# The transposed r and k of the last eight units: 32-by-32 blocks loaded by DMA and turned on VectorE in place of turns on TensorE

## The chip, the cores and the metric

The kernel runs on one core of one Trainium2 chip. Its time is the device time of one execution in microseconds (us); lower is better. Before the change the median of three runs is 600.69 us (600.6 to 601.51).

## What is computed

The reference is a recurrent attention layer, followed by a two-layer block with the activation h - tanh(h). All data is float32: 4 batches, 8 heads, 768 steps, head size 48; the model width is 8 x 48 = 384 and the hidden width 2048.

```python
for t in range(S):
    kt, vt, rt = (k[:, :, t], v[:, :, t], r[:, :, t])
    cur = np.einsum('bhd,bhe->bhde', u[None] * kt, vt)
    y[:, :, t] = np.einsum('bhd,bhde->bhe', rt, state + cur)
    state = w[None, :, :, None] * state + np.einsum('bhd,bhe->bhde', kt, vt)
x = y.transpose(0, 2, 1, 3).reshape(B * S, H * D)
h = x @ w_in
return (h - np.tanh(h)) @ w_out
```

## The kernel before

**Units.** The attention is cut into 24 units. A unit is 64 steps of two of the four batches (all heads), so its rows fill 128 partitions: two halves of 64 steps. Units alternate between the two pairs of batches. `unit(n)` describes one of them. Its steps, with lines of the profile: load r, k and v (`fetch`, L752, on SP's queue); kw = k times a table of decay (L893, VectorE); turn r and kw on TensorE into PSUM, so that features lie on partitions (`turn`, L764, four transposes of 128x128 for each, two heads at a time); take them out of PSUM as rT (times a table of decay, `scale_r`, L768, VectorE) and kT (`copy_k`, L777, ScalarE); rk = r k u and its sum over features, du (L781, L908, L785, VectorE), which ScalarE writes on the diagonal of the tile `at` (L789); rT against the state (`from_state`, L719 through `put`); rT against kT (`levels`, L719), whose part below the diagonal VectorE copies into `at` (L918); `at` against v into y and kw against v into the new state (`outputs`, L719); y out of PSUM into the tiles xt and rest (`to_xt`, `to_rest`, L855, ScalarE); the state's update and decay (`keep` L882, L927, VectorE). GpSimd moves `rest` to its rows of xt by small DMAs (`fill`, L876).

**Late units.** The last eight units, 16 to 23 (`two`, n >= L * (FIRST + 2)), have no PSUM bank of their own for the turned r and k and for the levels. There all of it shares the tile `yk_ps` with y and the new state. So the turns of a late unit come after everything that the unit before has in `yk_ps` was read (`free`: xt, rest, add, cp, diag of the unit before).

**Dense tiles.** Two units make a block j of 256 rows of the second part; there are 12 blocks, each with 8 tiles of 256 hidden columns. A tile is: h (L168, TensorE, twelve matmul records of the profile), five functions on ScalarE (L177 to L185), four steps on VectorE (`g` L192, c1 L194, c2 L196, cp L198), and the product with w_out. From the last pass of the first blocks on, that product is done with seven half-size products in place of eight: GpSimd forms sums of g (`sums_of_g`, L242 to L246), TensorE multiplies (`products`, L257), VectorE combines (`collect`, L285). The first six blocks (FIRST) go through the hidden columns in three passes; between passes their partial results wait in the twelve `part` tiles (L224), until `gather` (L289) adds them in. The other six blocks go through in one pass, among the late units.

**The order.** The program is one list per engine, in an order that a planner (`Plan`) makes when the kernel is built. Each step is a task with an engine, a cost, the tasks it comes after and a due time. `forward` plays the plan, `backward` finds the latest times, and a random search moves due times: first 2500 tries on the part up to BUSY = 240 us, then 500 tries on the whole (L470 to L486). The plan decides the order only; at run time each engine goes through its list and waits on semaphores.

Of the kernel before, what the change touches and what calls it, by code (L numbers as in the profile page):

```python
# [11 lines left out]
F32 = mybir.dt.float32  # L12
# [4 lines left out]
ALU = mybir.AluOpType  # L17
# [13 lines left out]
SHORT = 64  # L31
# [3 lines left out]
L = 2  # L35
FIRST = 6
# [19 lines left out]
class Dims:  # L56
    def __init__(self, r, moe_w_in):
        self.B, self.H, self.S, self.D = r.shape
        self.DM, self.DFF = moe_w_in.shape
        self.NP = self.H // 2  # L60
        self.NCH = self.S // C
        self.NU = self.NCH * self.B
        self.NK = self.DM // 128
        self.NX = self.D // self.NK
        self.NF = self.DFF // 128
        self.NT = L * C
        self.NB = self.NU // L

        self.HEAD = [slice(i * PAD, i * PAD + self.D) for i in range(2)]
# [76 lines left out]
class Dense:  # L146


    def __init__(self, nc, work, gpool, ps_d, shared, out, rows, outs=None, last=None, seven=None):
        self.nc, self.work, self.gpool, self.ps_d, self.new_outs, self.seven = nc, work, gpool, ps_d, outs, seven  # L150
        self.out, self.rows, self.xts, self.sums, self.last, self.negative = out, rows, {}, {}, last, set()
        self.d, self.w_in_sb, self.w_out_sb, self.m1b, self.smallb = (
            shared[x] for x in ("dims", "w_in", "w_out", "m1b", "smallb"))
# [55 lines left out]
    def empty(self, t, i):  # L209

        whole, at = t.fs[1] == self.d.NF, (t.j, i)
        if t.fs[0]:
            t.o = part = self.sums.pop(at) if whole else self.sums[at]
            if whole and t.j == self.d.NB - 1 and self.last is not None:
                t.o = self.last[:, i]
            if i and whole and t.j in self.negative:
                self.nc.vector.tensor_tensor(t.o, part, self.outs[i], ALU.subtract)
            else:
                self.nc.vector.tensor_tensor(t.o, self.outs[i], part, ALU.add)
            return  # L220
        if whole:
            t.o = self.work.tile([128, self.d.DM], F32, name="o", tag="o")
        else:
            t.o = self.sums[at] = self.work.tile([128, self.d.DM], F32, name="part", tag="part", bufs=L * FIRST)  # L224
        if t.j == self.d.NB - 1:
            if self.last is not None:
                t.o = self.last[:, i]
            self.nc.vector.tensor_copy(t.o, self.outs[i])
        else:
            self.nc.scalar.copy(t.o, self.outs[i])  # L230
# [70 lines left out]
class Plan:  # L301
# [10 lines left out]
    BEGIN = {"PE": 1.5, "DVE": 2.2, "ACT": 1.2, "POOL": 4.3, "SP": 1.2}  # L312

    def __init__(self):
        self.tasks, self.fills = [], []

    def add(self, engine, cost, run, after=(), due=1e9, data=0, gated=False, steps=0):
        t = SimpleNamespace(engine=engine, cost=cost, run=run, after=[x for x in after if x], due=due, data=data,
                            gated=gated, steps=steps, then=[], n=len(self.tasks))
        for x in t.after:  # L320
            x.then.append(t)
        self.tasks.append(t)
        return t

    def hop(self, t, x):
        return self.NEAR_HOP if x.engine == t.engine else self.HOP
# [94 lines left out]
    def backward(self, plan):  # L421
# [25 lines left out]
                    changed.add(x.engine)  # L447
        return latest

    def order(self, first=2500, tries=500):  # L450


        due = [t.due for t in self.tasks]
        for t in reversed(self.tasks):
            for x in t.then:
                due[t.n] = min(due[t.n], due[x.n] - t.cost - self.HOP - (self.LANDS if t.data else 0))
        plan = self.forward(due)
        for _ in range(4):
            due = self.backward(plan)
            plan = self.forward(due)  # L460
        chance = Random(5)

        def moved():
            by, at, wide = chance.choice((0.3, 1, 2, 5)), chance.uniform(0, until), chance.choice((15, 40, 100, 700))
            return [x + chance.gauss(0, by) * (start is not None and abs(start - at) < wide / 2) for x, start in zip(due, plan[1])]


        until = self.BUSY
        plan = self.forward(due, until)
        for _ in range(first):  # L470
            new = moved()
            other = self.forward(new, until)
            if other[0] <= plan[0]:
                plan, due = other, new
        plan = self.forward(due)
        until = plan[0]
        for _ in range(tries):
            new = moved()
            other = self.forward(new)
            if chance.random() < .5:  # L480
                latest = self.backward(other)
                again = self.forward(latest)
                if again[0] < other[0]:
                    other, new = again, latest
            if other[0] <= plan[0]:
                plan, due = other, new  # L486
        self.due = due
        _, starts, done = plan
        self.forward(due)
        fitted, order = {n: (free, runs) for free, n, runs in self.fitted}, []  # L490
        for t in done:
            t.start = starts[t.n]
            free, runs = fitted.get(t.n, (0.0, [])) if t.engine == "PE" else (0.0, [])
            order += [SimpleNamespace(engine="PE", cost=0.0, start=free, run=run) for run in runs]
            order.append(t)
        return order
# [19 lines left out]
def near(ctx, tc, r, k, v, w, u, out, shared, moe_w_in, moe_w_out):  # L516


    nc = tc.nc
    V, A, T, G, Q = nc.vector, nc.scalar, nc.tensor, nc.gpsimd, nc.sync  # L520
    d = shared["dims"]
# [12 lines left out]
    def fixed(name, shape, dt=F32):  # L534
# [2 lines left out]
    plan = Plan()  # L537
    add = plan.add
    e_of = {"SP": Q, "ACT": A, "PE": T, "DVE": V, "POOL": G}
    dense = Dense(nc, work, gpool, ps_d, shared, out,  # L540
                  lambda n: [(n % 2 * 2 + z) * d.S + n // 2 * SHORT for z in range(2)], lambda t: new_outs(t), shared["last"])
    HALF = [slice(z * SHORT, (z + 1) * SHORT) for z in range(2)]


# [178 lines left out]
    def unit(n):  # L723
# [46 lines left out]
        def scale_k():  # L770
            t.kT = work.tile([128, NP, 2, SHORT], F32, name="kT", tag="kT")
            V.tensor_tensor(t.kT, k_ps.rearrange("d (p z t) -> d p z t", p=NP, z=2),
                            inverse[:, :, None, 1:].to_broadcast([128, NP, 2, SHORT]), ALU.mult)

        def copy_k():
            t.kT = work.tile([128, NP, 2, SHORT], F32, name="kT", tag="kT")
            A.copy(flat4(t.kT), k_ps)  # L777
# [112 lines left out]
        if two:  # L890
            free = [b1.xt, b1.rest, b1.add, b1.cp, b1.diag]
        x.turn = add("PE", .46, lambda: turn(rt, r_ps), [x.r] + free, steps=8)
        x.kw = add("DVE", .47, lambda: V.tensor_tensor(kw[:, :, :D], t.kt[:, :, :D], w_down, ALU.mult), [x.k, downs, b2.out])  # L893
        x.turn_k = x.rk = add("PE", .46, lambda: turn(t.kt if direct else kw, k_ps), [x.k if direct else x.kw] + free, steps=8)
        both = [x.turn, x.turn_k]
        x.rT = add("DVE", .62, scale_r, both + [ups])
        if direct:
            x.kT = add("DVE", .62, scale_k, both + [inverted])
            x.extra = add("POOL", .5, thirds, [x.v])
        else:  # L900
            x.kT = add("ACT", .5, copy_k, both)
        if product:
            now = add("ACT", 1.05, own_k, [x.kT, w_us])
            x.own = add("PE", .7, own_levels, [now, x.rT, b2.out], steps=64)
            x.diag = add("DVE", .64, lambda: V.copy_predicated(t.at, same.bitcast(I32)[:, None, None, :].to_broadcast([128, 2, NP, SHORT]), own_lev), [x.own, b2.out])
        else:
            x.rk = add("DVE", .47, own, [x.r, x.k, b2.du, b1.rk if not b1.own else None])
            now = add("DVE", .47, lambda: V.tensor_tensor(t.rk, t.rk, ub, ALU.mult), [x.rk, bonus])  # L908
            x.du = add("DVE", .47, own_sum, [now, b2.diag])
            now = add("ACT", 1.0, lambda: diagonal(range(0, H // 2)), [x.du, b2.out])  # L910
            x.diag = add("ACT", 1.0, lambda: diagonal(range(H // 2, H)), [now])
# [20 lines left out]
                                for kk in range(NK) for i in range(2)]  # L932


    tiles, stored = [], {}
    mixed = []

    def mixing():
# [86 lines left out]
    for part in PASSES:  # L1025
        for j in range(FIRST):
            for f in range(done, done + part, 2):
                pace = 5.2 + (14.8 / part if not done and j < FIRST - 1 else 1.25)
                hidden(j, (done, done + part), f, now, pace, done >= SEVEN)
                now += pace  # L1030
        done += part
    for n in range(L * (FIRST + 2), d.NU):
# [327 lines left out]
```

## Time and profile before

| what | before |
|---|---|
| median of three runs | 600.69 us |
| the profiled execution | 599.5 us |
| its span, first to last instruction | 597.7 us |
| L764 from 354.8 us on (the late units' turns), records | 64, 0.272 us each |
| L768 from 357.6 us on (rT of late units) | 8, 0.692 us |
| L777 from 357.0 us on (kT of late units) | 8, 0.585 us |
| L671 (reciprocal of the table, once) | 1.778 us |
| loads of r, k, v on SP (L752), shortest and median issue of r | 0.595, 0.626 us |
| r, k, v loads, issue to landing, median | 2.9, 3.4, 3.5 us |
| xt fills on GpSimd's queue, issue to landing, median | 2.2 us |

An engine's busy time is the sum of its records. Matmuls overlap in the array, so a record's length is more than what one costs in a row of them. "Idle before, releaser" gives what ended an engine's wait. `PEld` is the weight load of TensorE, which shows a wait of TensorE first. The stretches used below count from the span's start.

### The profile page before, as it was taken

How to read it: one execution, taken by the hardware profiler on the slowest of the kernel's cores; microseconds unless marked ns; L12 is line 12 of the kernel's file. 1: busy time of each engine (PE TensorE's matmuls, PEld its weight loads, DVE VectorE, ACT ScalarE, POOL GpSimd, SP SyncE). 2: the span in 40 equal slices, each digit the busy share in tenths (PEclk: the TensorE clock that was granted, in tenths of full speed). 3: DMA queues.
4: the chain of work that ended last, by engine and by line, in shares of the span. 5: the costliest groups of instructions: out<-in, count | busy, mean ns of one | idle time of the engine just before them, and what ended most of it. 6: DMA issues, size and time to landing. Idle time of an engine off the chain costs nothing.

```text
span 597.7 us, 14262 instructions
## 1 busy us (share of the span) xinstructions
PE 579.0 (97%) x5589; PEld 491.5 (82%) x5589; DVE 465.6 (78%) x781; ACT 403.0 (67%) x902; POOL 203.7 (34%) x366
## 2 busy tenths in 40 slices
PE   8879999999999999999999999999999999999996
PEld 5557677777777779899999999989889888999995
DVE  5799979999999999986777775665776775555765
ACT  3798798899668867766555563765675866556552
POOL 5002212201000324454555463442435354334620
PEclk9999999999999999999999999999999999999999
DMA  6976986935211311201110011120211200100101
GB/s 127 228 132 121 168 195 110 142 94 114 60 53 27 62 29 24 50 5 24 28 26 13 16 28 34 34 47 15 55 22 27 42 1 9 27 2 7 27 3 31
DMA packets 86325, 33.77 MB, mean 56 GB/s; under 512 B 78536, under 2 KB 80680, under 8 KB 86248
## 3 DMA queue, kind: packets, MB, share of 16 engines
q1 hardware_dynamic: 81084, 25.57, 22.0%
q0 software_dynamic: 4992, 6.99, 5.5%
q8 instruction: 46, 0.75, 0.6%
q14 instruction: 31, 0.25, 0.1%
q10 hardware_dynamic: 172, 0.20, 0.1%
HBM read 26.94 MB, written 4.72 MB: 53 GB/s over the span
## 4 chain that ended last, share of the span: by engine, by line
PE 72%; DVE 14%; ACT 5%; issue 4%; DMA 3%; SPq 2%; DVEq 0%; POOL 0%; ACTq 0%; POOLq 0%
PE h L168 34%; PE p L257 25%; PE o L206 5%; PE yk_ps L719 5%; SPq L752 2%; DVE tg L196 2%; DVE tg L194 1%; DVE g L192 1%; DVE g L198 1%; DMA vt<-in_v_dram 1%; PE yk_ps L764 1%; ACT at L789 1%; DMA kt<-in_k_dram 1%; DVE rT L768 1%; DVE mixed L266 1%
## 5 line engine op out<-in xcount | busy, mean ns | idle before, releaser
L168 PE MATMUL h<-xt,w_in_sb 128*128 128x256 f32 x1152 | 281.1, 381 | 1.9 <-DVE w_in_sb L143 0.9
L168 PEld LDWEIGHTS h<-xt,w_in_sb 128*128 128x128 f32 x1152 | 212.5, 190 | 32.7 <-DVE g L192 1.4
L242 POOL TENSOR_TENSOR sg<-g 128x256 f32<-128x256 f32 x69 | 53.1, 770 | 171.4 <-DVE g L198 105.3
L194 DVE SCALAR_TENSOR_TENSOR tg<-s,tg 128x512 f32<-128x512 f32 x96 | 69.5, 723 | 53.5 <-ACT tg L181 28.6
L257 PE MATMUL p<-mixed,sg 128*128 128x192 f32 x426 | 104.0, 326 | 0.0
L181 ACT ACTIVATE tg<-h 128x512 f32<-128x512 f32 x96 | 57.2, 596 | 55.7 <-PE h L168 55.7
L192 DVE TENSOR_TENSOR g<-h,th 128x512 f32<-128x512 f32 x96 | 66.0, 688 | 26.8 <-ACT tg L181 10.6
L177 ACT ACTIVATE s<-h 128x512 f32<-128x512 f32 x96 | 57.4, 598 | 41.4 <-PE h L168 41.3
L876 POOL DMA_DIRECT2D xt<-rest x66 | 32.3, 495 | 142.7 <-ACT rest L855 142.7
L179 ACT ACTIVATE th<-h 128x512 f32<-128x512 f32 x96 | 57.4, 598 | 33.4 <-PE h L168 33.2
L198 DVE COPY_PREDICATED g<-small,tg 128x512 f32<-128x512 int32 x96 | 75.6, 787 | 4.0
L196 DVE SCALAR_TENSOR_TENSOR tg<-q,tg 128x512 f32<-128x512 f32 x96 | 68.2, 711 | 9.8 <-ACT q L183 7.4
L257 PEld LDWEIGHTS p<-mixed,sg 128*128 128x128 f32 x426 | 75.0, 190 | 0.0
L206 PE MATMUL o<-w_out_sb,g 128*128 128x384 f32 x192 | 69.8, 490 | 1.7 <-DVE g L198 1.6
L257 PE MATMUL p<-w_out_sb,g 128*128 128x192 f32 x284 | 71.2, 332 | 0.0
L183 ACT ACTIVATE q<-s,m1b 128x512 f32<-128x512 f32 x96 | 69.7, 726 | 0.7
L185 ACT ACTIVATE small<-s,smallb 128x512 f32<-128x512 f32 x96 | 69.4, 723 | 0.3
L257 PEld LDWEIGHTS p<-w_out_sb,g 128*128 128x128 f32 x284 | 51.8, 190 | 7.1 <-DVE o L285 0.2
L789 ACT ACTIVATE at<-same,du 128x64 f32<-128x64 f32 x184 | 47.7, 342 | 5.3 <-DVE du L785 5.0
L206 PEld LDWEIGHTS o<-w_out_sb,g 128*128 128x128 f32 x192 | 35.5, 190 | 18.4 <-issue 1.9
L244 POOL TENSOR_TENSOR sg<-sg,g 128x128 f32<-128x128 f32 x69 | 43.2, 626 | 5.1
L246 POOL TENSOR_TENSOR sg<-sg,g 128x128 f32<-128x128 f32 x69 | 36.9, 534 | 5.1
(132 smaller groups left out, 688.2 us busy)
## 6 DMA issues: line engine op xcount, KB each, us to landing
st<-in_moe_w_out_dram SPq DMA_DIRECT2D x8, 768.0 KB, 5.0
rt<-in_r_dram SPq DMA_DIRECT2D x48, 96.0 KB, 2.9
vt<-in_v_dram SPq DMA_DIRECT2D x48, 96.0 KB, 3.5
st<-in_moe_w_in_dram SPq DMA_DIRECT2D x16, 288.0 KB, 5.4
kt<-in_k_dram SPq DMA_DIRECT2D x44, 96.0 KB, 3.4
out_dram<-o POOLq DMA_DIRECT2D x44, 96.0 KB, 2.1
st<-in_moe_w_in_dram POOLq DMA_DIRECT2D x16, 96.0 KB, 4.8
xt<-rest POOLq DMA_DIRECT2D x66, 16.0 KB, 2.2
```

The costliest lines, as they stand in the source:

```text
L168: self.nc.tensor.matmul(t.h2[:, z], self.w_in_sb[:, t.f // 2, kk, z * 128 : (z + 1) * 128], self.xts[t.j][:, kk].rearrange("p b t -> p (b ...
L177: A.activation(out, t.h, AF.Square)
L179: A.activation(out, t.h, AF.Tanh)
L181: A.activation(out, t.h, AF.Tanh, scale=G1)
L183: A.activation(out, t.s, AF.Square, bias=self.m1b)
L185: A.activation(out, t.s, AF.Relu, bias=self.smallb, scale=-1.0)
L192: V.tensor_tensor(t.g, t.h, t.th, ALU.subtract)
L194: V.scalar_tensor_tensor(t.tg, t.s, C4, t.tg, ALU.mult, ALU.mult)
L196: V.scalar_tensor_tensor(t.tg, t.q, K1, t.tg, ALU.add, ALU.mult)
L198: V.copy_predicated(t.g, t.small.bitcast(I32), t.tg)
L206: self.nc.tensor.matmul(self.outs[i], t.g2[:, z, i * C : (i + 1) * C], self.w_out_sb[:, t.f + z, :], start=t.first and z == 0, stop=t.last ...
L257: self.nc.tensor.matmul(ps[bank][:, half * n : (half + 1) * n], a, b, start=t.first and half == 0, stop=t.last, skip_group_check=True)
```

## The change

A planned task can now be changed after the first search: `Plan.change` notes new fields for it. `order` first makes the plan as before, with the old tasks. Then it puts the changes in, takes new due times for what starts after BUSY = 240 us, and searches again for 500 tries with only those due times moving.

For late units four tasks are changed:

- The turn of r and the turn of kw on TensorE become `spread_out` on SP: eight DMAs for each, which load r, or k itself, in blocks of 32 features by 32 steps. Heads are split into 32 and 16 features, so the pieces are 128 or 64 bytes long. The blocks lie where the partial sums of the first blocks lay, in one tile `parts` that takes the place of the twelve `part` tiles; a unit uses one of two sets.
- rT becomes, on VectorE, a transpose of the 32-by-32 blocks (128x512) and a multiplication by the decay table.
- kT moves from ScalarE to VectorE: a transpose of the blocks of k and a multiplication by the inverse table, since k comes without the decay. The inverse table is made once more, at unit 16, in `parts`.

The loads of r, k and v for rk, kw and the outputs stay as they are. rT and kT of a late unit no longer come out of `yk_ps`; they come after the levels of the unit before, whose buffers they follow.

```diff
 class Plan:
+    def change(self, t, **new):
+        self.changes.append((t, new))
...
     def order(self, first=2500, tries=500):
...
+        self.search(due, tries, chance, 0.0)
+        for t, new in self.changes:
+            for x in t.after:
+                x.then.remove(t)
+            vars(t).update(new)
+            t.after = [x for x in t.after if x]
+            for x in t.after:
+                x.then.append(t)
+        for _ in range(4):
+            plan = self.forward(self.due)
+            latest = self.backward(plan)
+            self.due = [old if start < self.BUSY else new for old, new, start in zip(self.due, latest, plan[1])]
+        plan = self.search(self.due, tries, chance, self.BUSY)
...
+    parts = const.tile([128, L * FIRST, d.DM], F32, name="parts", tag="parts")
...
+    spread = parts.rearrange("q a n -> q (a n)")
+    blocks = [spread[:, i * 512 : (i + 1) * 512].rearrange("q (x b e) -> q x b e", x=2 * NP, b=SHORT // 32) for i in range(4)]
+    again = spread[:, 2048 : 2048 + NP * (SHORT + 1)].rearrange("d (p n) -> d p n", p=NP)
...
+        def spread_out(src, i):
+            heads = src[half * 2 : half * 2 + 2, :, steps_at, :].rearrange("z (p h) t d -> h t (z p) d", h=2)
+            for q in range(4):
+                h, e = divmod(q, 2)
+                wide = min(32, D - 32 * e)
+                for b in range(SHORT // 32):
+                    Q.dma_start(out=blocks[n % 2 * 2 + i][q * 32 : (q + 1) * 32, :, b, :wide],
+                                in_=heads[h, b * 32 : (b + 1) * 32, :, e * 32 : e * 32 + wide])
+
+        def across(name, i, by):
+            out = work.tile([128, 2, NP, SHORT], F32, name=name, tag=name)
+            V.transpose(out.rearrange("d z p t -> d (z p t)"), blocks[n % 2 * 2 + i].rearrange("q x b e -> q (x b e)"))
+            V.tensor_tensor(out, out, by[:, None].to_broadcast([128, 2, NP, SHORT]), ALU.mult)
+            return out.rearrange("d z p t -> d p z t")
...
+        def across_k():
+            if n == L * (FIRST + 2):
+                V.reciprocal(again, power)
+            t.kT = across("kT", 1, again[:, :, 1:])
...
         x.turn = add("PE", .46, lambda: turn(rt, r_ps), [x.r] + free, steps=8)
+        if two:
+            freed = [tiles[y].o for y in parted[:4]] if n < L * (FIRST + 3) else []
+            plan.change(x.turn, engine="SP", cost=4.8, run=lambda: spread_out(r, 0), after=[b2.rT, *freed], data=.8, steps=0)
...
+        if two:
+            plan.change(x.turn_k, engine="SP", cost=4.8, run=lambda: spread_out(k, 1), after=[b2.kT, *freed], data=.8, steps=0)
...
+        if two:
+            plan.change(x.rT, cost=1.22, run=across_r, after=[x.turn, b1.lev])
+            plan.change(x.kT, engine="DVE", cost=1.22 + (1.75 if n == L * (FIRST + 2) else 0), run=across_k, after=[x.turn_k, b1.lev])
```

More of the change, by code (lines that the diff above doesn't have):

```diff
@@ L146, with __init__ @@
 class Dense:
-    def __init__(self, nc, work, gpool, ps_d, shared, out, rows, outs=None, last=None, seven=None):
+    def __init__(self, nc, work, gpool, ps_d, shared, out, rows, outs=None, last=None, seven=None, parts=None):
         self.nc, self.work, self.gpool, self.ps_d, self.new_outs, self.seven = nc, work, gpool, ps_d, outs, seven
+        self.parts = parts
         self.out, self.rows, self.xts, self.sums, self.last, self.negative = out, rows, {}, {}, last, set()
@@ L223, in empty @@
         else:
-            t.o = self.sums[at] = self.work.tile([128, self.d.DM], F32, name="part", tag="part", bufs=L * FIRST)
+            t.o = self.sums[at] = self.parts[:, L * t.j + i]
         if t.j == self.d.NB - 1:
@@ L314, in __init__ @@
     def __init__(self):
-        self.tasks, self.fills = [], []
+        self.tasks, self.fills, self.changes = [], [], []
     def add(self, engine, cost, run, after=(), due=1e9, data=0, gated=False, steps=0):
@@ L448, in backward, with moved, search @@
         return latest
+    def moved(self, due, plan, chance, begin, until):
+        by, at, wide = chance.choice((0.3, 1, 2, 5)), chance.uniform(begin, until), chance.choice((15, 40, 100, 700))
+        return [x + chance.gauss(0, by) * (start is not None and start >= begin and abs(start - at) < wide / 2) for x, start in zip(due, plan[1])]
+    def search(self, due, tries, chance, begin):
+        plan = self.forward(due)
+        span = plan[0]
+        for _ in range(tries):
+            new = self.moved(due, plan, chance, begin, span)
+            other = self.forward(new)
+            if chance.random() < .5:
+                latest = self.backward(other)
+                if begin:
+                    latest = [y if start < begin else x for x, y, start in zip(latest, new, other[1])]
+                again = self.forward(latest)
+                if again[0] < other[0]:
+                    other, new = again, latest
+            if other[0] <= plan[0]:
+                plan, due = other, new
+        self.due = due
+        return plan
     def order(self, first=2500, tries=500):
@@ L460, in order @@
             plan = self.forward(due)
[L461 to L468, printed above, removed]
+        chance, until = Random(5), self.BUSY
         plan = self.forward(due, until)
         for _ in range(first):
-            new = moved()
+            new = self.moved(due, plan, chance, 0.0, until)
             other = self.forward(new, until)
@@ L474, in order @@
                 plan, due = other, new
[L475 to L487, printed above, removed]
+        self.search(due, tries, chance, 0.0)
[11 more added lines that the diff above has]
+        plan = self.search(self.due, tries, chance, self.BUSY)
         _, starts, done = plan
-        self.forward(due)
+        self.forward(self.due)
         fitted, order = {n: (free, runs) for free, n, runs in self.fitted}, []
@@ L539, in near @@
     e_of = {"SP": Q, "ACT": A, "PE": T, "DVE": V, "POOL": G}
+    parts = const.tile([128, L * FIRST, d.DM], F32, name="parts", tag="parts")
     dense = Dense(nc, work, gpool, ps_d, shared, out,
-                  lambda n: [(n % 2 * 2 + z) * d.S + n // 2 * SHORT for z in range(2)], lambda t: new_outs(t), shared["last"])
+                  lambda n: [(n % 2 * 2 + z) * d.S + n // 2 * SHORT for z in range(2)], lambda t: new_outs(t), shared["last"], parts=parts)
+    spread = parts.rearrange("q a n -> q (a n)")
+    blocks = [spread[:, i * 512 : (i + 1) * 512].rearrange("q (x b e) -> q x b e", x=2 * NP, b=SHORT // 32) for i in range(4)]
+    again = spread[:, 2048 : 2048 + NP * (SHORT + 1)].rearrange("d (p n) -> d p n", p=NP)
     HALF = [slice(z * SHORT, (z + 1) * SHORT) for z in range(2)]
@@ L773, in scale_k, with across_r @@
                             inverse[:, :, None, 1:].to_broadcast([128, NP, 2, SHORT]), ALU.mult)
+        def spread_out(src, i):
[11 more added lines that the diff above has]
+            return out.rearrange("d z p t -> d p z t")
+        def across_r():
+            t.rT = across("rT", 0, power[:, :, :SHORT])
+        def across_k():
+            if n == L * (FIRST + 2):
+                V.reciprocal(again, power)
+            t.kT = across("kT", 1, again[:, :, 1:])
         def copy_k():
@@ L932, in unit @@
                                 for kk in range(NK) for i in range(2)]
-    tiles, stored = [], {}
+    tiles, stored, parted = [], {}, []
     mixed = []
@@ L1029, in near @@
                 hidden(j, (done, done + part), f, now, pace, done >= SEVEN)
+                if done + part == d.NF and f + 2 == d.NF:
+                    parted.append(len(tiles) - 1)
                 now += pace
```

## The prediction

> **What bounds the kernel now.** I read the page's busy shares first, then stretches of the late part, then what TensorE waits for there, and last single instructions in order of time. Times are of the profiled execution before the change.
>
> ```profile
> PE 579.0 (97%) x5589; PEld 491.5 (82%) x5589; DVE 465.6 (78%) x781; ACT 403.0 (67%) x902; POOL 203.7 (34%) x366
> ```
>
> ```profile
> 300.00:360.00 60.00, 59.90 (x355) 55.96 (x354) 44.38 (x74) 35.34 (x65) 31.26 (x50) 1.00 0.11 24
> 360.00:420.00 60.00, 59.90 (x530) 55.23 (x529) 36.15 (x61) 34.56 (x80) 24.01 (x41) 1.00 0.15 29
> 420.00:480.00 60.00, 60.00 (x667) 53.55 (x666) 44.09 (x75) 42.31 (x103) 25.32 (x44) 1.00 0.18 36
> 480.00:540.00 60.00, 59.58 (x606) 53.52 (x605) 34.58 (x55) 36.16 (x82) 25.80 (x46) 1.00 0.04 10
> ```
>
> The columns of the stretches are PE, PEld, DVE, ACT and POOL busy, granted clock, DMA share, GB/s. The changed units run from 355 to 521 us. TensorE is full there at full clock; VectorE has 114.8 of 180 us busy from 360 to 540, so 65 us free, and DMA is under 0.2. A busy PE can hide waits between overlapping records, so I also read what the weight loads wait for from 240 us to the end (us in total, times, longest):
>
> ```profile
> PEld yk_ps L719 <- issue: 4.2, 16, 0.3
> PEld h L168 <- DVE g L192: 1.4, 2, 1.0
> PEld yk_ps L719 <- DVE rT L768: 0.9, 2, 0.5
> PEld yk_ps L719 <- DVE at L918: 0.8, 3, 0.3
> PEld yk_ps L719 <- ACT kT L777: 0.7, 1, 0.7
> ```
>
> All rows of that answer come to 9.4 us in 358; 4.5 us of it is "issue" at the small matmuls, which stays. What better order could win is the other 4.9 us. So the late part is TensorE's own work, placed back to back, and TensorE time taken out comes off the end almost whole. The turns, in order of time (start, length):
>
> ```profile
> 388.05 1.24 PE L168 MATMUL h<-xt,w_in_sb 128*128 128x256 f32 x5
> 389.13 0.60 PE L764 MATMUL yk_ps<-ident,kw 128*128 128x128 f32 x4
> 389.57 0.60 PE L764 MATMUL yk_ps<-ident,rt 128*128 128x128 f32 x4
> 390.00 1.46 PE L168 MATMUL h<-xt,w_in_sb 128*128 128x256 f32 x6
> 391.57 0.69 PE L719 MATMUL yk_ps<-rT,state 48*64 48x64 f32 x32
> ```
>
> Four turns are 0.60 us as a record, but what follows starts after 0.44 and 0.43 us. The step from start to start is their price, 0.435 us, not the record's length.
>
> [...]this trace has 272 ns each, and shows that the pipelined cost is 109 ns. [...]this trace has only 192-byte pieces for r, k and v, none of 64 bytes.
>
> **The change part by part.**
>
> *TensorE.* For units 16 to 23, two groups of four turns go: 16 x 0.435 = **7.0 us** off TensorE. Nothing is added; the built order shows the same counts of all other matmuls. Bounds: 16 x 0.43 = 6.9 to 16 x 0.44 = 7.0.
>
> *ScalarE* loses eight copies of kT (L777, 0.585 us each, 4.7 us), off the path.
>
> *VectorE.* Per unit: two block turns and two products by a table replace one product (L768). The price of a 512-wide VectorE instruction, again from start to start (end of the run, nothing between):
>
> ```profile
> 587.34 0.69 DVE L194 SCALAR_TENSOR_TENSOR tg<-s,tg 128x512 f32<-128x512 f32 x1 [1.45 <-ACT tg L181]
> 587.95 0.69 DVE L192 TENSOR_TENSOR g<-h,th 128x512 f32<-128x512 f32 x1
> 588.55 0.68 DVE L196 SCALAR_TENSOR_TENSOR tg<-q,tg 128x512 f32<-128x512 f32 x1
> ```
>
> That is 0.61 us. For a turn I take the same[...]. So 4 x 0.61 - 0.61 = 1.83 us a unit, 14.6 for eight[...]; one reciprocal (L671's twin, 1.78 us) is added near 305 us. All of it fits in the 65 free us and the 15.6 free from 300 to 360. Without that cover it would cost its full 14.6 us: that is the slower rival. With it, the cost is delay: a dense tile's `g`, c1, c2 and cp stand in line behind a turn. Before, 57 unit instructions on VectorE after 240 us (at 8, rT 8, rk 14, du 7, kw 7, state 13) go with 1.4 + 0.9 + 0.8 = 3.1 us of TensorE waiting for VectorE, 0.054 us each. 24 more make **+1.3 us** (0 to 4).
>
> *The waits that go.* rT and kT can now be made before the unit's turn at the yk_ps bank comes, as they no longer come out of it. In the built order kT and rT of unit 16 stand on VectorE before unit 16's first matmul by several tiles. The waits on rT (0.9) and on kT (0.7 at the loads, of which 0.4 shows on PE itself) go: **-1.3 us**. What is late next is the bank: from_state of n+1 waits for to_xt, to_rest and keep of n (about 0.97 + 0.65 + 0.56 us after the outputs). In the built order the tightest place, unit 22 to 23, has six h matmuls and six products between (1.29 + 0.97 = 2.3 us) and no keep there, 1.6 us plus hops: even. Before, the turn waited for the same things.
>
> *SP and the DMA engines.* 128 DMAs are added, 16 a unit, each of 256 pieces of 128 or 64 bytes. Issue time by number of pieces: 144, 256 and 512 pieces (ns, shortest/median/longest[...]):
>
> ```profile
> L123 SPq DMA_DIRECT2D st<-in_moe_w_in_dram x16: 311/458/4207, 11.0 to 144.2; - x16
> L123 SPq DMA_DIRECT2D st<-in_moe_w_out_dram x8: 385/480/3486, 21.2 to 164.9; - x8
> ```
> ```profile
> L752 SPq DMA_DIRECT2D rt<-in_r_dram x48: 595/626/1676, 2.1 to 453.0; - x48
> ```
>
> I take 0.5 us (0.4 to 0.63). A unit needs 16 x 0.5 + 6 x 0.63 = 11.8 us of SP; units follow each other every (521.2 - 358.4) / 7 = 23 us, and 21 in the new order. SP becomes the bound only above (21 - 3.8) / 16 = 1.08 us an issue. The spread loads of n wait for the turns of n-2, and behind them on SP stand rt, kt and vt of later units; the last half of v for unit 23 is the very last. There is most of a unit's time for each, so I cost this at nothing. The first spread loads wait until the partial sums that lay there are gathered (L289, first at 249.6 us, last at 345.6, twice a block): block 2's is at about 288, unit 16 begins near 350. If one came late, a unit would wait 16 x 0.5 + 2.9 us, 11 us, once. Packets: queue 1 took 7.6% of 16 engines from 360 to 530 us for 12,686 packets, 16 ns each; 32,768 more are 33 us of all 16 engines in some 230 us. POOL's xt fills (2.2 us to landing) share them[...].
>
> *The order.* Up to about 240 us it is the same on the compute engines. After it a second search of 500 tries works on the late part alone. It can win at most the 4.9 us named; 1.3 are counted. I take **-0.8** (0 to -3).
>
> *Sum:* -7.0 + 1.3 - 1.3 - 0.8 = -7.8 us. The profiled execution took 599.5 us (597.7 span and 1.8 around it): 591.7. The median of the runs, 600.69, lies 1.2 above it: **592.9**.
>
> **The rivals.** (1) *Part is given back*: turns of 1.2 us, late fills or the bank make TensorE wait 3 to 5 us more. For: VectorE [...]gets 24 more instructions. Against: 0.054 us an instruction so far. 596.5 (595 to 599.4). (2) *The search tidies up*: the remaining waits fall by 3 us more: 589.9. For: 4.9 us are there. Against: the first search left them. (3) *Slower, VectorE becomes the bound among the units*: each added VectorE us shows on TensorE: 600.7 + 14.6 - 9.1 (turns, waits, search) = 606.2. It decides once more than 10.3 of the 14.6 us show (9.1 and the 1.2 of 0.2%), seven tenths; the 65 free us speak against. That turns stay on TensorE is excluded by the built order.
>
> **How the numbers follow.** Forecast (590.3 to 595) 0.65, rival 1 0.20, rival 2 0.08, rival 3 and any late queue 0.07. The range 589.5 to 597.5 leaves out rival 3, a third of 1 and under half of 2, 0.17. Within 0.2% (1.2 us, what a measurement can tell from no change) lies the top of rival 1, 0.03; faster 0.90, slower 0.07.
>
> **What would show it.** L764 has no instruction after 240 us; between the first and last late unit TensorE is 59.5 or more of 60; waits of L719 on rT and kT are gone; the block turns last about 0.7 us; SP issues under 0.7 us. Wrong if TensorE's waits after 240 us grow beyond 12 us, naming `g`, cp or POOL's sums (rival 1 or 3), or if DMA appears in them.

## The result and the profile after

The changed kernel takes 591.57 us in the median (591.32 to 592.05), beside 600.85 us (600.6 to 601.51) for the kernel before in the same comparison: a ratio of 0.9845 (95% interval 0.9828 to 0.9862), 9.3 us less. The forecast was 592.9. The profiled execution took 591.6 us, its span is 589.5 us.

The page's busy shares of the kernel after:

```profile
PE 571.2 (97%) x5525; PEld 485.0 (82%) x5525; DVE 484.1 (82%) x806; ACT 398.9 (68%) x894; POOL 208.3 (35%) x366
```

TensorE has 64 instructions fewer, VectorE 25 more and 18.5 us more to do (16 turns and 16 products of 0.70 us, less eight products of 0.69, and one reciprocal of 1.76). ScalarE has lost its eight copies.

The stretches of the late part of the kernel after (PE, PEld, DVE, ACT and POOL busy, granted clock, DMA share, GB/s):

```profile
300.00:360.00 60.00, 60.00 (x378) 55.64 (x377) 52.63 (x86) 34.53 (x64) 31.58 (x48) 1.00 0.22 41
360.00:420.00 60.00, 59.99 (x638) 54.69 (x638) 46.86 (x74) 39.31 (x97) 28.63 (x45) 1.00 0.33 56
420.00:480.00 60.00, 60.00 (x629) 53.93 (x628) 46.58 (x79) 37.95 (x87) 28.07 (x46) 1.00 0.21 36
480.00:540.00 60.00, 60.00 (x490) 54.80 (x489) 37.55 (x59) 37.85 (x83) 28.17 (x51) 1.00 0.05 11
```

TensorE is as full as before, at full clock: so most of the time that went is work it no longer has. VectorE is busy for 131.0 of the 180 us from 360 on, 16.2 more than before, and still has 49 us free. The DMA share has doubled from 360 to 420 us.

What the weight loads of the kernel after wait for from 240 us on (us in total, times, longest):

```profile
PEld yk_ps L750 <- issue: 4.5, 17, 0.3
PEld p L207 <- DVE e L286: 0.5, 1, 0.5
PEld yk_ps L750 <- ACT s L178: 0.5, 2, 0.2
PEld yk_ps L750 <- DVE state L937: 0.4, 1, 0.4
```

All rows come to 7.3 us, 9.4 before. Waits on rT and kT are gone from the list, and nothing with a DMA has come in. The 1.4 us for `g` at h are gone too.

The blocks in the tile `parts`, kernel after (ns shortest/median/longest, first and last start):

```profile
L813 SPq DMA_DIRECT2D parts<-in_r_dram x64: 314/449/2026, 273.3 to 475.1; - x64
...
L818 DVE STREAM_TRANSPOSE kT<-parts x8: 647/697/707, 316.2 to 499.9; 128x512 f32<-128x512 f32 x8
...
DMA to landing us min/median/max: 1.7/2.0/3.6
```

The turns lie from 316 to 500 us; the first matmul of a unit that uses them starts from 2 us (units 21 and 23) to 28 us (unit 16) after the last of its turns has started. A block load issues in 0.449 us in the median.

**Where the time went.** One landmark divides each trace: the start of the first half-size product from `w_out_sb` (L258, L257 before). Up to it the compute engines have the same order in both kernels. It starts at 225.4 us before and 226.4 after: VectorE is level in both up to 19 us, and then waits 1.07 us for a piece of w_in that it didn't wait for in the execution before. From the landmark to the end of the span it is 372.3 us before and 363.1 after: 9.2 us less. Of these the turns are 7.0 (64 at 109 ns, the step of before), the weight loads' waits 9.4 - 7.3 = 2.1, and 0.1 is left over.

### The profile page after: what moved, and what is told of

It reads as the page before. It is cut to its first block, busy times and chain, and to the rows that moved or that the text cites. A ratio compares the mean times of both kernels' runs of the same rounds, so it can differ in the third digit from the quotient of the medians.

```text
span 589.5 us, 14312 instructions
## 1 busy us (share of the span) xinstructions
PE 571.2 (97%) x5525; PEld 485.0 (82%) x5525; DVE 484.1 (82%) x806; ACT 398.9 (68%) x894; POOL 208.3 (35%) x366
## 4 chain that ended last, share of the span: by engine, by line
PE 76%; DVE 11%; ACT 4%; issue 3%; DMA 3%; SPq 2%; POOL 0%; DVEq 0%; ACTq 0%; POOLq 0%
PE h L169 37%; PE p L258 27%; PE o L207 5%; PE yk_ps L750 5%; SPq L783 2%; DMA st<-in_moe_w_in_dram 2%; DVE tg L197 1%; DVE g L193 1%; DVE tg L195 1%; DVE g L199 1%; DVE rT L799 1%; ACT at L844 1%; ACT s L178 1%; PE x_ps L795 1%; DMA kt<-in_k_dram 1%
## 5 line engine op out<-in xcount | busy, mean ns | idle before, releaser
L258 PE MATMUL p<-mixed,sg 128*128 128x192 f32 x426 | 104.0, 326 | 0.0
L195 DVE SCALAR_TENSOR_TENSOR tg<-s,tg 128x512 f32<-128x512 f32 x96 | 68.3, 712 | 25.9 <-ACT tg L182 13.8
L258 PEld LDWEIGHTS p<-mixed,sg 128*128 128x128 f32 x426 | 75.1, 190 | 0.0
L258 PE MATMUL p<-w_out_sb,g 128*128 128x192 f32 x284 | 71.1, 332 | 0.0
L258 PEld LDWEIGHTS p<-w_out_sb,g 128*128 128x128 f32 x284 | 52.5, 190 | 7.4
L245 POOL TENSOR_TENSOR sg<-sg,g 128x128 f32<-128x128 f32 x69 | 44.6, 647 | 5.1
L247 POOL TENSOR_TENSOR sg<-sg,g 128x128 f32<-128x128 f32 x69 | 39.0, 566 | 5.1
```

The lines of the kernel that those rows point to most:

```text
L195: V.scalar_tensor_tensor(t.tg, t.s, C4, t.tg, ALU.mult, ALU.mult)
L258: self.nc.tensor.matmul(ps[bank][:, half * n : (half + 1) * n], a, b, start=t.first and half == 0, stop=t.last, skip_group_check=True)
```

## The experiments

Theory A is the forecast's: TensorE's time for the turns is the gain, a better order adds about one us, VectorE and SP hide what they get. Rival B: the second search is the gain, the blocks only make room for it. Rival C: rT and kT that no longer wait for the bank are a large part. Rival D: the added work on VectorE or on SP is at its limit, and a little more of it is slower. "Order kept" means that the planner sees the changed kernel's tasks and costs, so the edit comes into the order that the changed kernel has. Each kernel was timed beside the kernel before on the same chip (600.5 to 601.05 us).

The last two columns are from each profiled execution: landmark to end (the "late part"), and all waits of weight loads from 240 us on. In every row the median less the late part is 227.8 to 228.9 us, so what differs between the kernels lies in the late part.

| kernel | median us (range) | ratio to before | late part us | waits us |
|---|---|---|---|---|
| before | 600.85 (600.6–601.51) | 1 | 372.3 | 9.4 |
| after | 591.57 (591.32–592.05) | 0.9845 (0.9828–0.9862) | 363.1 | 7.3 |
| second search alone | 599.78 (598.68–600.61) | 0.9986 (0.9979–0.9992) | 371.4 | 8.7 |
| no second search | 592.54 (592.23–592.68) | 0.9863 (0.9848–0.9878) | 363.6 | 7.8 |
| TensorE turns again | 599.06 (597.99–599.52) | 0.9968 (0.9956–0.998) | 370.2 | 6.5 |
| only r in blocks | 596.84 (595.82–597.47) | 0.9929 (0.9916–0.9943) | 368.3 | 9.2 |
| rT, kT after the bank | 592.2 (591.69–592.62) | 0.9857 (0.9842–0.9873) | 363.8 | 7.9 |
| turn twice, order kept | 596.99 (596.89–597.59) | 0.9941 (0.9927–0.9954) | 368.5 | 12.8 |
| turn twice, planned | 591.73 (591.24–591.85) | 0.9847 (0.9834–0.9861) | 363.0 | 7.1 |
| turn four times, planned | 599.08 (598.62–600.24) | 0.9975 (0.9965–0.9985) | 370.6 | 14.8 |
| loads twice, six units, order kept | 602.76 (601.99–604.16) | 1.0034 (1.002–1.0047) | 375.0 | 16.8 |
| loads twice, four units, order kept | 600.97 (599.76–602.32) | 1.0009 (1.0002–1.0016) | 372.5 | 14.1 |
| loads twice, four units, planned | 591.37 (590.85–591.83) | 0.9849 (0.9835–0.9863) | 363.0 | 7.1 |
| search of 1500 tries | 591.91 (591.65–593.0) | 0.9858 (0.9843–0.9872) | 363.7 | 7.9 |

### What the change gives: turns or search

**The second search alone.** The tasks stay as before; only the late due times are searched again.

```diff
-        for t, new in self.changes:
+        for t, new in []:
```

> The second search of the late part is done, but no task is changed: the turns stay on TensorE, rT and kT come out of the bank as before. Theory: the search alone wins 0.8 us (0 to 2), so 599 to 600.8 us. Rival, that the search is most of the gain beyond the turns: 2 us or more, under 598.9 us. 64 turns after 240 us are there again.

Measured: 0.14% less (0.08 to 0.21%), 0.7 us by the medians. **No second search**, with the tasks changed:

```diff
-        plan = self.search(self.due, tries, chance, self.BUSY)
+        plan = self.search(self.due, 0, chance, self.BUSY)
```

> The tasks are changed and take new due times once, but no second search follows. Theory: the 7.0 us of turns are there without a search, and early rT and kT save the rest, so it gives back 1 us at most 3: 592.5 to 594.5 us. Rival, that the search is needed to place VectorE's added instructions: over 597 us, with TensorE waiting for VectorE.

592.54: 8.3 of the 9.3 us are there without a second search. The ranges of the times don't touch (592.23 and 592.05), though the intervals of the ratios overlap. By the late parts the search is worth 0.9 us alone and 0.5 with the tasks changed, by the medians 0.7 and 1.0: some 0.5 to 1 us, as A says. B falls.

**The turns again.** In the order of the changed kernel, each late unit does eight turns of the identity into the bank ahead of `from_state`. Their results aren't used; r and k still come by blocks.

```diff
         def from_state():
+            if two:
+                for bank in (r_ps, k_ps):
+                    for p in range(NP):
+                        T.transpose(bank[:, p * C : (p + 1) * C], ident, ident)
```

> The changed kernel in its own order, with eight turns of the constant identity put on TensorE in front of each late unit's from_state; their results are not used. If the gain is TensorE's time (my theory), it gives back 16 x 0.435 = 7.0 us: 598.5 us, and the waits stay near those of the changed kernel. If the gain came from the waits and the new order (rival), TensorE has room and the time stays under 594 us. If both halves matter alike, about 596 us.

599.06, 7.5 us over the changed kernel. One stretch of it, and the longest single wait of its weight loads:

```profile
360.00:420.00 60.00, 60.00 (x614) 54.79 (x613) 46.77 (x73) 36.59 (x91) 28.46 (x45) 1.00 0.34 56
```
```profile
PEld p L207 <- DVE e L286: 0.5, 1, 0.5
```

TensorE is full as before, all waits are 6.5 us (0.8 below after), and the late part is 7.1 us longer. The sum of the waits didn't grow, so the 7 us are the matmuls' own time. The edit brings back the work of the turns and not their chain, as no rT or kT is made from them: what the bank's chain cost isn't tested here, but only the other 1.8 of the 9.3 us are left for it and for the search.

**Only r in blocks.** k stays on TensorE and ScalarE.

```diff
-            plan.change(x.turn_k, engine="SP", cost=4.8, run=lambda: spread_out(k, 1), after=[b2.kT, *freed], data=.8, steps=0)
+            pass
...
-            plan.change(x.kT, engine="DVE", cost=1.22 + (1.75 if n == L * (FIRST + 2) else 0), run=across_k, after=[x.turn_k, b1.lev])
```

> Only r is loaded in blocks and turned on VectorE; kw is turned on TensorE and kT copied by ScalarE as before, so the bank's chain of turn, copy and from_state stays for k. Theory, the gain is TensorE's time: half of the 7.0 us, the search's 1 us and half of the rest, about 596 us (595.3 to 596.8). Rival, that freeing the bank of both is what counts: 598 us or more. Second rival, that VectorE's added work costs about 2 us in the changed kernel and half of it is spared here: under 595.3 us.

596.84, just over the 595.3 to 596.8 expected: 5.3 us are given back, more than half of the 9.3. The late part is 5.2 us longer: half of the turns, 3.5, and 1.9 more of waits (9.2 for 7.3). The longest of these is one of 1.5 us on a sum of `collect`. It ends at 248 us, ahead of all late units, so it comes from this order and not from k's turns; whether another order would avoid it wasn't tried.

**rT and kT after the bank.** They wait for the same reads of the unit before as the old turns did, though they don't use the bank.

```diff
-            plan.change(x.rT, cost=1.22, run=across_r, after=[x.turn, b1.lev])
+            plan.change(x.rT, cost=1.22, run=across_r, after=[x.turn, b1.lev] + free)
...
-            plan.change(x.kT, engine="DVE", cost=1.22 + (1.75 if n == L * (FIRST + 2) else 0), run=across_k, after=[x.turn_k, b1.lev])
+            plan.change(x.kT, engine="DVE", cost=1.22 + (1.75 if n == L * (FIRST + 2) else 0), run=across_k, after=[x.turn_k, b1.lev] + free)
```

> rT and kT of a late unit are planned only after the unit before has left the bank, as its turns had to be before; all else as in the changed kernel. Theory, early rT and kT are worth the 1.3 us of waits that went: 592.5 to 594 us. Rival, that the new order wins nothing from the early start: 591.6 us within 0.5. Second rival, that the early start is what makes room for VectorE's added time: over 595 us.

592.2, just above the first rival's 591.6 within 0.5: 0.6 us more by the medians, 0.7 in the late part, and the ranges overlap. It is also about as much as one planned order differs from another: the kernels below that hide added work, and the one with a longer search, lie from 591.37 to 591.91. So the early start is worth some 0.6 of the 9.3 us, if anything. C falls.

### Where the room on VectorE ends

**Each turn twice, order kept.** The planner isn't told, so the second turn pushes aside whatever stands behind.

```diff
-            V.transpose(out.rearrange("d z p t -> d (z p t)"), blocks[n % 2 * 2 + i].rearrange("q x b e -> q (x b e)"))
+            for _ in range(2):
+                V.transpose(out.rearrange("d z p t -> d (z p t)"), blocks[n % 2 * 2 + i].rearrange("q x b e -> q (x b e)"))
```

> The changed kernel in its own order, with each of the 16 block turns on VectorE done twice, which adds 16 x 0.61 = 9.8 us of VectorE time among the late units. Theory, VectorE has room and each instruction costs TensorE 0.054 us: +0.9 us, 592.5 us (592 to 594). Rival, VectorE is near the bound and most of the added time shows: +5 to +10 us, 597 to 601 us.

596.99, so the theory's 592 to 594 is missed: 5.4 us for 16 turns, 0.34 us each, where one takes 0.71 us. The waits of weight loads in this kernel:

```profile
PEld yk_ps L750 <- DVE state L938: 1.9, 2, 1.7
PEld yk_ps L750 <- ACT small L186: 1.6, 1, 1.6
PEld yk_ps L750 <- DVE at L982: 1.3, 1, 1.3
PEld p L258 <- DVE e L286: 1.3, 1, 1.3
```

The longer waits are a few, on whatever VectorE made late: the state, `at`, a sum of `collect`. The one put down to ScalarE's `small` is at a `from_state` that starts at 474.81, and the rT which that reads, with its turn doubled, is done at 474.66, within 0.2 us of `small`. All waits come to 12.8 us, 5.5 over after, which is the whole loss. Does this say that VectorE is full? The next kernel differs from this one only in what the planner knows: **each turn twice, planned**, with the cost of rT and kT raised from 1.22 to 1.82.

```diff
-            plan.change(x.rT, cost=1.22, run=across_r, after=[x.turn, b1.lev])
+            plan.change(x.rT, cost=1.82, run=across_r, after=[x.turn, b1.lev])
-            plan.change(x.kT, engine="DVE", cost=1.22 + (1.75 if n == L * (FIRST + 2) else 0), run=across_k, after=[x.turn_k, b1.lev])
+            plan.change(x.kT, engine="DVE", cost=1.82 + (1.75 if n == L * (FIRST + 2) else 0), run=across_k, after=[x.turn_k, b1.lev])
```

> Each block turn on VectorE twice as in the run with the order kept (which gave 597.0 us, 5.4 more than the changed kernel), but the planner is told the cost, 0.6 us more a task, and searches with it. If VectorE has room and the order alone was wrong for it (my theory now): 592 to 594 us. If VectorE's time is short among the late units whatever the order (rival): 596 us or more.

591.73, the changed kernel's time, with VectorE at 495.5 us busy and waits of 7.1 us. Its fullest stretch among the late units:

```profile
360.00:420.00 60.00, 60.00 (x662) 54.02 (x660) 53.22 (x82) 38.31 (x95) 28.72 (x43) 1.00 0.34 55
```

So VectorE isn't full; the loss of the unplanned kernel was a matter of place. **Four turns, planned** (`range(4)`, cost 3.02):

> Each block turn on VectorE four times, planned at 3.02 us a task in place of 1.22: 48 more turns, 29 us of VectorE time, where twice (planned) cost nothing: 591.7 us. VectorE has 52 us free from 360 to 540 us in the changed kernel's records. If the planner can fill that room: under 593.5 us. If the room that can be used ends before: 595 us or more; the more TensorE waits for VectorE the nearer its end.

599.08: this order doesn't hide it. Two stretches of the kernel with four turns, and the wait of its weight loads that goes with dense tiles:

```profile
360.00:420.00 60.00, 58.25 (x652) 52.34 (x651) 54.40 (x84) 36.58 (x92) 27.44 (x43) 1.00 0.28 43
420.00:480.00 60.00, 58.30 (x594) 52.50 (x593) 56.60 (x94) 35.44 (x82) 25.73 (x44) 1.00 0.29 50
```
```profile
PEld h L169 <- DVE g L193: 2.2, 3, 1.1
```

VectorE is busy for 54.4 and 56.6 of 60 us, and TensorE for 58.3 in both. All waits are 14.8 us, 7.5 over after, and the late part is 7.5 us longer. In the changed kernel VectorE stands at 47 of 60 in both stretches, and in the planned kernel with two turns at 53 and 49. Two rivals to "the room ends" stand untested: one task now holds VectorE for 3.6 us on end (rT from 406.81 to 410.39 us: four turns, 2.94, and the product), and what stands behind it in the list starts after that even where there is room on the whole, and a longer search might place the same work better.

### Where the room on SP ends

**Each block load twice, units 18 to 23, order kept.** The second copy goes to another part of `parts`. For unit 18 (copies issued from 317 to 336 us) it overwrites partial sums of the first blocks that are still to be gathered (the last at 345.7 us), so these rows of the output are other numbers; the work is the same.

```diff
                     Q.dma_start(out=blocks[n % 2 * 2 + i][q * 32 : (q + 1) * 32, :, b, :wide],
                                 in_=heads[h, b * 32 : (b + 1) * 32, :, e * 32 : e * 32 + wide])
+                    if n >= L * (FIRST + 3):
+                        Q.dma_start(out=extra_blocks[n % 2 * 2 + i][q * 32 : (q + 1) * 32, :, b, :wide],
+                                    in_=heads[h, b * 32 : (b + 1) * 32, :, e * 32 : e * 32 + wide])
```

> The changed kernel in its own order, but each block load of units 18 to 23 is issued twice, the second time to rows that nothing reads: 96 more DMAs on SP, 32 x 0.48 + 6 x 0.63 = 19 us of SP a unit against some 22 us between units. Theory, loads are a unit ahead and SP and the DMA engines cover it: 591.6 us (up to 593, where two units stand close). Rival, block loads are nearly late: 595 us or more, with TensorE or VectorE waiting for DMAs of parts.

602.76, slower than the kernel before: 11.2 us over the changed kernel. The theory is wrong; the rival has the time right, but named the wrong wait, for the blocks. This is what VectorE waits for longest (us in total, times, longest), and behind the longest of these waits the weight load of a product waits 8.2 us:

```profile
DVE rk L840 <- DMA kt<-in_k_dram: 16.9, 3, 10.0
```

That raises two questions: which transfer is late, and is it the amount or the place? **The same for units 20 to 23 only, order kept** (`n >= L * (FIRST + 4)`), 64 more DMAs, overwrites nothing that is used.

> As the run with the block loads twice (602.8 us), but only for units 20 to 23 (64 more DMAs in place of 96), again in the changed kernel's own order. In that run VectorE waited 2.7, 4.2 and 10.0 us for loads of k that stand behind the block loads on SP, and the last of these fell on TensorE. If the queue is the cause (my theory now), the same place is late here, by about as much less as fewer loads stand before it: 593 to 600 us, VectorE waiting at rk for kt. If the cause was that run's overwritten partial sums or the DMA engines' load (rivals), about 591.6 us, or waits for parts.

600.97: 9.4 us over the changed kernel, and more than the 593 to 600 expected. Here the chain is short enough to read in order of time. SP's queue, VectorE and TensorE of this kernel (start, length, idle before and its releaser):

```profile
421.58 0.45 SPq L817 DMA_DIRECT2D parts<-in_k_dram  x1
...
424.16 1.27 SPq L784 DMA_DIRECT2D kt<-in_k_dram  x2
```
```profile
427.81 0.56 DVE L840 TENSOR_TENSOR rk<-rt,kt 128x384 f32<-128x384 f32 x1 [8.59 <-DMA kt<-in_k_dram]
...
428.88 0.35 DVE L286 TENSOR_TENSOR e<-e,p 128x192 f32<-128x192 f32 x1
```
```profile
429.29 1.01 PE L258 MATMUL p<-w_out_sb,g 128*128 128x192 f32 x2 [6.40 <-DVE e L286]
```

The late transfer isn't a block. It is the ordinary load of k, which stands on SP behind 32 block loads and is issued at 424.16. rk of that unit, 23, stands in VectorE's list at 419.2 and waits 8.59 us; behind it stand c2 of a tile and `e` of `collect`, and for that the product waits. In the changed kernel the same load is issued at 410.60 (SP's queue, then VectorE, of the kernel after):

```profile
401.82 4.86 SPq L813 DMA_DIRECT2D parts<-in_k_dram  x8
...
410.60 1.28 SPq L783 DMA_DIRECT2D kt<-in_k_dram  x2
```
```profile
419.74 0.55 DVE L836 TENSOR_TENSOR rk<-rt,kt 128x384 f32<-128x384 f32 x1
```

From the issue's end, 411.9, to rk, 419.74, are 7.9 us; 2.8 us go to the landing (the median of the five loads of r, k and v issued from 406 to 412 us), so the slack is some 5 us. The loads of k for units 21 and 22 have about the same. With the loads doubled, unit 22's rk waits 3.8 us too, but TensorE feels nothing of it: not every late load costs.

The stall is 6.4 us for the matmul and 6.8 for the weight load; the late part is 9.4 us longer. The rest is in the stretches around it (four-unit kernel, columns as above):

```profile
420.00:425.00 5.00, 2.89 (x15) 2.31 (x13) 0.00 (x0) 2.04 (x4) 0.00 (x0) 1.00 0.45 67
425.00:430.00 5.00, 0.71 (x2) 0.72 (x3) 2.19 (x5) 0.87 (x2) 0.00 (x0) 0.73 0.32 59
430.00:433.00 3.00, 3.00 (x10) 2.70 (x10) 2.86 (x8) 0.00 (x0) 2.81 (x5) 0.50 0.14 31
433.00:436.00 3.00, 3.00 (x15) 2.63 (x14) 1.95 (x3) 0.00 (x0) 1.87 (x4) 0.81 0.44 100
```

TensorE's work ends at 422.9 (429.29 less the 6.40). The granted clock is 1.00 up to 425 us and 0.73 in the mean of the next five; after the stall TensorE is busy at 0.50, and it is back at 1.00 from 436 us on. What that costs shows in the products, two at 0.50 and two at 1.00 (start, length):

```profile
430.73 0.85 PE L258 MATMUL p<-mixed,g 128*128 128x192 f32 x2
431.37 0.85 PE L258 MATMUL p<-mixed,sg 128*128 128x192 f32 x2
...
437.27 0.49 PE L258 MATMUL p<-mixed,g 128*128 128x192 f32 x2
437.59 0.49 PE L258 MATMUL p<-mixed,sg 128*128 128x192 f32 x2
```

They step by 0.64 and by 0.32 us. The four products and six records of h from 429.29 to 434.35 take 5.06 us, the same from 436.62 to 439.21 take 2.59: 2.5 us are lost. That and the 6.8 make 9.3 of the 9.4. In the kernel with unplanned turns, whose longest wait is 1.7 us, the granted clock is 1.00 in each stretch of 60 us from 300 to 540.

**The same 64 DMAs, planned**, with SP's cost of a group raised from 4.8 to 9.6:

```diff
-            plan.change(x.turn, engine="SP", cost=4.8, run=lambda: spread_out(r, 0), after=[b2.rT, *freed], data=.8, steps=0)
+            plan.change(x.turn, engine="SP", cost=9.6 if n >= L * (FIRST + 4) else 4.8, run=lambda: spread_out(r, 0), after=[b2.rT, *freed], data=.8, steps=0)
...
-            plan.change(x.turn_k, engine="SP", cost=4.8, run=lambda: spread_out(k, 1), after=[b2.kT, *freed], data=.8, steps=0)
+            plan.change(x.turn_k, engine="SP", cost=9.6 if n >= L * (FIRST + 4) else 4.8, run=lambda: spread_out(k, 1), after=[b2.kT, *freed], data=.8, steps=0)
```

> The same 64 more DMAs, but the planner is told 9.6 us of SP for a task that it was told 4.8 for, and searches with it. If only the order on SP's queue was wrong for the added loads (theory): under 593 us. If SP or the DMA engines have no more room among the late units, whatever the order (rival): 595 us or more.

591.37, the changed kernel's time, 9.6 us under the same DMAs in the old order. In its trace the k load and rk of unit 23 stand at:

```profile
420.30 1.27 SPq L784 DMA_DIRECT2D kt<-in_k_dram  x2
```
```profile
443.38 1.08 DVE L840 TENSOR_TENSOR rk<-rt,kt 128x384 f32<-128x384 f32 x1
```

The issue ends at 421.6 and rk runs 21.8 us later, with no wait for a DMA. That SP or the DMA engines had no capacity left for these loads falls with this run. D falls in both halves where the planner knows of the doubled work, and comes true, by 5.4 and 9.4 us, where it doesn't.

**A longer second search**, 1500 tries (`3 * tries`):

> The changed kernel with 1500 tries in the second search in place of 500. Waits of TensorE after 240 us are 7.4 us, 4.8 of them issue, so at most 2.6 us are left. Theory: 0 to 1 us, 590.6 to 591.6 us. Rival, the order is still loose: under 590 us. It may also be no better than the plan's own error: up to 592.3 us.

591.91: nothing gained. No version tried is distinctly faster than the changed kernel; the 591.37 with doubled loads lies within 0.2 us of it, and their ranges overlap.

## Why the prediction was right

Mechanism and direction hold. The sum was -7.8; measured are -9.3 by the medians and -9.2 by the late parts. The 1.2 us by which the profiled execution before lay under its median were rightly added: it reached the landmark at 225.4 us, earlier than any other kernel's trace here (225.8 to 227.4).

- **TensorE, -7.0: right.** Undoing it alone costs 7.5 us by the median and 7.1 in the late part. The step from start to start, not the 0.60 us record, was the price. Sixteen such records would be 9.6 us, near the whole gain of 9.3, so the total alone couldn't have told the two prices apart.
- **VectorE's delay, +1.3: the term that was mis-sized.** It measured about 0, the lower end of its range. The sum without it is -9.1. The waits put down to VectorE, rT's left out, came to 3.1 us before and 1.8 after, and to 1.7 without the second search. The waits of weight loads other than "issue" fell from 4.9 to 2.5 us, by 2.4, where my terms let them fall by 0.8 net (1.3 + 0.8 - 1.3). The step that failed is "0.054 us each. 24 more make +1.3": an average over waits that the planner had left is no price for an instruction which it places itself. Sixteen more turns cost nothing measurable when planned and 0.34 us each when not; neither is 0.054. It wasn't a price per instruction at all.
- **The turn's duration, 0.61 us: too low.** It was my estimate, the step of other VectorE instructions on 128x512; the 1.2 us of rival 1 was a guess. What follows a turn starts 0.68 to 0.74 us after it; the record is 0.70. This made VectorE 16.2 us busier from 360 to 540 us, not 14.6, at no cost. The slower rival had each added VectorE us show on TensorE; the kernel with two planned turns has 29.9 us more on VectorE than the kernel before (495.5 for 465.6) and shows none of it. With two turns it is busy for up to 53.2 us of 60 among the late units without loss, with four for 54.4 to 56.6 with loss; that the busy share alone sets the point isn't shown.
- **The waits on rT and kT, -1.3: the size holds in the list, the reason only partly.** They are gone from it, but making rT and kT wait for the bank again costs 0.6 to 0.7 us, not clear of noise.
- **The second search, -0.8: right** (0.7 to 0.9 alone, 0.5 to 1.0 in the changed kernel).
- **SP and the DMA engines, nothing: right in time, thin in its cover.** Issues took 0.449 us (I took 0.5), a unit's 16 come to 3.99 + 3.89 = 7.9 us. "Most of a unit's time for each" was wrong for the loads of k: for units 21 to 23 they have 5 us of slack before rk, because they stand behind two groups of blocks. I had named rt, kt and vt behind the groups, but priced the stall as a late group. With the loads doubled it is a late k, 8.6 us on VectorE and 6.8 on TensorE, once. That nothing came late in the changed kernel is the planner's doing, which counts SP's time; the forecast's own reason for it didn't hold for k. The packets took 12.1% of the DMA engines from 240 us to the end (4.5% before): 26 us of all 16 for 35,499 more, 12 ns each, where I took 33 us at 16 ns.
- **The bank:** "even" held. The state is in the list for 0.4 us, once.

Open is where the early start of rT and kT went: the waits on them are gone in the changed kernel, and the 0.6 us that they cost when brought back can't be told from nothing here.

## What to carry to other kernels

When TensorE is full and nothing waits long, price a matmul that goes by its step from start to start, and take it off the end whole (7.0 us forecast here, 7.1 to 7.5 measured); for what moves to another engine, ask how full that engine will be in that stretch, not what a mean wait per instruction was. An in-order queue has two limits, how much and where: the same doubled work cost 5.3 us on VectorE and 9.6 us on SP in an order made without it, and nothing in one made with it. Before calling an added DMA free, find what is queued behind it and how long before its use that is issued: here it was a plain load of k with 5 us to spare.

## What the runs showed of the hardware

- A 32x32-block transpose of a 128x512 fp32 tile on VectorE has a record of 0.70 us (0.71 where repeated), and four in a row take 2.94 us, 0.74 a step; a 128x512 product of two tiles steps by 0.61.
- A DMA of 256 pieces of 128 or 64 bytes lands in 2.0 us in the median, sooner than the loads of r, k and v in 192-byte pieces (2.9 to 3.3 us over the whole span, 2.6 to 3.0 from 240 us on); it also has half as many pieces. In the stall above it was the issue, 0.45 us each on SP, that made a load late, not the landing: rk starts 2.4 us after the issue of its k load ends.
- After one stall of 6.4 us the granted clock was 0.50, and four products and six records of h took 5.06 us in place of the 2.59 at 1.00. So this late load cost 2.5 us more, over a third of its wait. In the six-unit kernel, after a stall of 7.8 us, 0.50 was granted from 430 to 436 us and as many matmuls took 4.64 us (432.52 to 437.16), 2.59 at 1.00 (439.43 to 442.02): 2.0 us more.
